# Two MoE layers behind attention: constant products at the layer border, GpSimd's weight splits moved to VectorE, the exact pass's condition moved forward, two copies per small block left out

## Chip, cores and metric

One core of a Trainium2 chip runs the whole program. The metric is the device time of one execution in microseconds (us); less is better. The kernel before was timed in three runs.

## What is computed

The reference, cut: causal attention over 4 x 12 heads of 448 tokens of width 64 gives a matrix x of 1792 tokens x 768. Two mixture-of-experts layers follow, each with 8 experts of a 768 x 1024 and a 1024 x 768 matrix.

```python
def moe(x, w_gate, w1, w2):            # first layer
    logits = x @ w_gate
    expert_idx = argmax(logits, axis=1)
    gate_w = softmax(logits)[arange(N), expert_idx]
    for e in range(E):
        mask = expert_idx == e
        out[mask] = gate_w[mask, None] * (relu(x[mask] @ w1[e]) @ w2[e])

def moe2(x, w_gate, w1, w2):           # second layer
    logits = x @ w_gate
    cap = N // E                       # 224 tokens an expert
    for idx in argsort(-logits.flatten()):
        tok, e = idx // E, idx % E
        if assigned[tok] >= 0 or counts[e] >= cap: continue
        assigned[tok] = e; counts[e] += 1
    for e in range(E):
        mask = assigned == e
        out[mask] = relu(x[mask] @ w1[e]) @ w2[e]
```

The second layer hands out tokens greedily, in the order of all 14336 logits, until each expert holds 224.

## The kernel before

The program has three stages on one core: `attention` (to about 225 us), `moe1` (the first layer, line 119 on) and `moe2` (the second layer, line 477 on).

**Weights.** Each float32 matrix is used as a sum of two parts in a reduced format: `split` (L171 and L172 in the first layer, L773 and L774 in the second) lets ScalarE copy a loaded 128-row chunk to a high part and another engine subtract it for the low part. A product of two such operands is three matmuls: high by high, high by low, low by high. The chunks are loaded by SyncE into 8 raw buffers; a split frees its buffer and issues the load of the chunk 8 further on. In `moe1` and in most of `moe2` VectorE does the subtraction. In `moe2` GpSimd does it for four chunks of the second matrix of the first expert in order (p = 0, odd k from KD on, L774).

**First layer.** Tokens are grouped by expert. A full block has 128 rows: `take` transposes gathered rows (with ScalarE and VectorE making the parts xh and xl of `xx`), `up`, `relu`, `transp_h`, `down`, and the tail functions `tail0` to `tail3` of the block before (logits for the next layer, scatter of its rows), which are issued between the products. How many rows an expert has is a value that all engines read, and blocks are behind conditions (L380, L387, L403). Where an expert leaves at most HB = 64 rows over, `small` (L305) is used. It holds 64 rows in 128 columns of the stationary operand: columns 0 to 63 the high part, columns 64 to 127 the low part, so that `pair` (L312) needs two matmuls where a block needs three, and `fold` and `transp_s` add the halves. The low part comes there by two VectorE copies at its start (L308, L309). `small` then issues weight splits by the list SPS = (5, 0, 2, 0, 3, 4, 0) between its pieces; the first five stand ahead of everything but the copies. In this trace it runs four times, from about 268, 394, 440 and 462 us.

**Border.** Ahead of the first layer nine matmuls of 512 columns with constant operands stand on TensorE (L417, `WARM`); their result is not used. Behind the last expert come the tails of the last block (L444 to L474), by which the second layer's logits get complete.

**Second layer.** The greedy order is found by thresholds: `search` (L627) takes four rounds for each expert in order, each a comparison on VectorE (`probe`, L622), 14 small matmuls (L665), a reduction (L666, L668), one matmul (L676) and the new thresholds; `assign` (L694) makes the index list of the expert by further small matmuls (L711, L725, L729). Both are one generator, `phases` (L735), whose pieces are placed by hand between the products: `go(n)` runs n pieces, `turn` runs one whenever the costs in the list `YY` say that it is due, `finish(p)` all that is left for an expert. For p = 0 nothing stands beside it but the first splits. Then `gather` (L781) fetches the expert's rows, `take` (L800) transposes them, `up4` (L822) makes the first four column tiles chunk by chunk as weights arrive, `up` (L815) the others, `relu` (L827, L828), `down` (L838), `put` (L785) scatters rows to the output. The splits of p + 1's first matrix and its `take` stand between the `down` products of p, by the list s0.

**Exact pass.** Ties can defeat the thresholds; each search adds to `bad` if so. At the very end VectorE turns `bad` into a flag (L918), every engine reads it (L921), and under a condition (L922) the whole layer is done again with exact ranks. The last output scatter, `put_half` (L791), is issued ahead of it.

The lines the text speaks of most:

```python
for s in (slice(0, 1), slice(1, KD)):                                             # L308
    nc.vector.tensor_copy(xh[:, s, HB:], xl[:, s, :HB])                           # L309
ops = [(o, a[:, k], wh, k == 0, k == n - 1), (o[:HB], a[:, k, :HB], wl, False, False)]
(nc.gpsimd if p == 0 and k >= KD and k % 2 else V).tensor_sub(l, r, h.bitcast(F32))  # L774
```

Of the kernel before, what the change touches and what calls it, by code (L numbers as in the profile page):

```python
# [119 lines left out]
def moe1(tc, w1, w2, wg, xs, y2, l2, ident, before, iob, cr, gt, g0, raw, early, iok, L, srch):  # L120
    nc = tc.nc
    with ExitStack() as c:
# [182 lines left out]
        def small(e, j):  # L305

            W = (w1h[e % 2], w1l[e % 2])
            for s in (slice(0, 1), slice(1, KD)):  # L308
                nc.vector.tensor_copy(xh[:, s, HB:], xl[:, s, :HB])  # L309
# [132 lines left out]
        for e in range(E):  # L442
            expert(e)

# [14 lines left out]
        tail1()  # L459
        for n in range(2):  # L460
            nc.tensor.transpose(pU[0][:, n * 128:n * 128 + 128], d[:, n:n + 1].to_broadcast([128, 128]), ident)
        tail2()

# [6 lines left out]
        tail3(False)  # L470
        V.tensor_mul(rh.rearrange("p (i e) -> p i e", e=E), oi[:, :, None].to_broadcast([128, NB, E]),
                     l2c[:, None, :].to_broadcast([128, NB, E]))
        nc.tensor.matmul(pU[1][:, :NB * E], hp, rh, start=True, stop=True)
        V.tensor_add(L, L, pU[1][:, :NB * E].rearrange("p (i e) -> p i e", e=E))  # L474


def moe2(tc, w1, w2, y2, out, ident, before, ones, io8, iok, iob16, L, srch, raw, force):
# [7 lines left out]
    with ExitStack() as c:  # L485
# [50 lines left out]
        iob = io8[:, None, :].to_broadcast([128, PT, E])  # L536

# [87 lines left out]
        def search(p):  # L625
# [61 lines left out]
            t = total()  # L687

# [6 lines left out]
        def assign(p):  # L695
# [14 lines left out]
            nc.tensor.matmul(t[:, :1], before, T["rt"], start=True, stop=True)  # L710
            V.tensor_copy(T["col"], t[:, :1])  # L711
# [14 lines left out]
            V.tensor_scalar(T["ev"], t[:16, :NA], float(N), None, op0=OP.min)  # L726
            yield YY[9]
# [67 lines left out]

        def take(kk):
            t = ps.tile([128, 512], F32, name="w", bufs=6)[:, :2 * CAP].rearrange("p (k g t) -> p k g t", k=2, g=2)
# [10 lines left out]
        def up(f, h):  # L808
            if h == 0:
                U[f] = ps.tile([128, 512], F32, name="w", bufs=6)[:, :CAP]  # L810
            u = U[f]
            fs = slice(f * 128, (f + 1) * 128)
            for k in range(3 * h, 3 * h + 3):
                for n, (w, x) in enumerate(((w1h, xh), (w1l, xh), (w1h, xl))):
                    nc.tensor.matmul(u, w[:, k, fs], x[:, k], start=(k == 0 and n == 0), stop=(k == KD - 1 and n == 2))  # L815

        def up4(k):
            for f in range(4):
                if k == 0:
                    U[f] = ps.tile([128, 512], F32, name="w", bufs=6)[:, :CAP]  # L820
# [11 lines left out]
        def down(g, hf, f0, f1):  # L832
            if f0 == 0:
                Y[0] = ps.tile([128, 512], F32, name="w", bufs=6)[:G2, :384]
# [19 lines left out]

        go(1)
        split(0, 0)
        go(2)
# [8 lines left out]
        for f in range(4, KF):  # L866
# [7 lines left out]
            split(0, KD + f)  # L874
        for p in range(E):
            early = p > 0 and p + 1 in done
            if p:
# [3 lines left out]
                for f in range(KF):  # L881
# [3 lines left out]
                    turn(p, 1)  # L885
                    relu(f)
# [3 lines left out]
            for g in range(2):  # L890
                for hf in range(2):
                    for f in range(0, KF, 2):
                        down(g, hf, f, f + 2)
                        turn(p, 1)
                        if n == s0[0]:
                            finish(p + 1)
                            flush()
                        if p + 1 in done and not early:
# [15 lines left out]
                if p < E - 1 or g == 0:  # L914
                    put(p, g)


        V.tensor_scalar(T["bi"], bad, 0.0, None, op0=OP.not_equal)  # L918
        if force:
            V.memset(T["bi"], 1)  # L920
        again = nc.values_load(T["bi"][0:1, 0:1], min_val=0, max_val=1)  # L921
        with tc.If(again > 0):  # L922
            reset()
            for p in range(E):
                best()
                V.tensor_tensor(T["eq"], T["lm"], T["m"][:, :, None].to_broadcast([128, PT, E]), op=OP.is_equal)
                V.tensor_mul(T["eq"], T["eq"], iob)
                V.tensor_reduce(T["mn"], T["eq"], axis=AX.X, op=OP.min)
                V.tensor_tensor(T["oh"], iob, T["mn"][:, :, None].to_broadcast([128, PT, E]), op=OP.is_equal)
                exact()  # L930
                owned()
                V.scalar_tensor_tensor(apen, T["asg"], -BIG, apen, op0=OP.mult, op1=OP.add)
                V.memset(T["fl"], 0.0)
                V.scalar_tensor_tensor(T["full"], cap, 0.0, left, op0=OP.is_equal, op1=OP.mult)
                for _ in assign(p):
                    pass
                gather(p)
                pend.clear()
                for k in range(NC):
                    load(p, k)  # L940
                    r = raw[(p * NC + k) % NR]
                    if k < KD:
                        h, l = w1h[:, k], w1l[:, k]
                    else:
                        r, h, l = r[:, :DM], w2h[:, k - KD], w2l[:, k - KD]
                    A.activation(h, r, AF.Copy)
                    V.tensor_sub(l, r, h.bitcast(F32))
                for kk in range(0, KD, 2):
                    take(kk)
                for f in range(KF):  # L950
                    up(f, 0)
                    up(f, 1)
                    relu(f)
                for g in range(2):
                    for hf in range(2):
                        down(g, hf, 0, KF)
# [339 lines left out]
```

## Time and profile before

| what | value |
|---|---|
| three runs | 986.0, 988.75, 988.78 us; median 988.75 |
| the profiled execution, its own time | 990.98 us |
| its span, first to last instruction | 989.1 us |
| mean granted TensorE clock over the span | 0.945 |
| busy: PE, PEld, DVE, ACT, POOL | 891.8, 744.1, 629.1, 503.1, 215.4 us |
| share of the chain that ended last: PE, DVE, DMA | 27%, 3%, 2% |

PE is TensorE's matmul pipe, PEld its weight loads, DVE VectorE, ACT ScalarE, POOL GpSimd, SP SyncE; a name with q is the engine's instruction queue. The durations are from one profiled execution, whose time is 1.9 us over its span. The chain's shares are of the whole span but the chain is followed back only to 625.87 us, so 27% of PE is most of what it covers. [...] Where a row says x8 it stands for eight instructions one after another; what stands in brackets is the idle time of the engine before it and what ended it.

### The profile page before, as it was taken

The page shows a single profiled execution, that of the slowest core. Times are in us where ns is not written, and L with a number is a line of the kernel's source. Part 1 is how long each engine was busy: PE and PEld are TensorE (multiplying, and loading weights), DVE is VectorE, ACT ScalarE, POOL GpSimd, SP SyncE. Part 2 cuts the span into 40 slices and gives each one's busy share as a digit, 9 for nine tenths or more (in the row PEclk, how much of TensorE's full clock was granted, in tenths as well). Part 3 has the DMA queues.
Part 4 walks back from the last instruction along what each step waited for, and adds up shares of the span by engine and source line. Part 5 has one row for each costly group of instructions (what it writes and reads, how often), then busy time and mean ns, then how long its engine had stood idle before and what let it go on. Part 6 is the DMA issues. An engine that isn't in the chain of part 4 may idle for free. (4 is left out here: it accounts for less than half of the span.)

```text
span 989.1 us, 18118 instructions
## 1 busy us (share of the span) xinstructions
PE 891.8 (90%) x6122; PEld 744.1 (75%) x6122; DVE 629.1 (64%) x1815; ACT 503.1 (51%) x1101; POOL 215.4 (22%) x244
## 2 busy tenths in 40 slices
PE   5999999995899996987999999458999999999993
PEld 3666666663778885766798878348899999999993
DVE  6888989868552613853821152578797887975640
ACT  5888888854563524654822253033444444445540
POOL 5555444404121111111211112104111011011001
PEclk9999999996999998998999999757999999999997
DMA  8654555706743803873831031074685766766701
GB/s 174 132 148 118 144 138 119 251 11 206 269 146 132 305 34 103 289 290 112 301 152 49 33 101 50 22 244 139 188 246 171 218 190 182 222 199 199 256 16 31
DMA packets 76911, 156.54 MB, mean 158 GB/s; under 512 B 30753, under 2 KB 41793, under 8 KB 76738
## 3 DMA queue, kind: packets, MB, share of 16 engines
q1 hardware_dynamic: 70514, 128.44, 42.2%
q0 software_dynamic: 6224, 26.11, 8.1%
q8 instruction: 70, 1.15, 0.5%
q14 instruction: 103, 0.84, 0.3%
HBM read 135.84 MB, written 18.67 MB: 156 GB/s over the span
## 5 line engine op out<-in xcount | busy, mean ns | idle before, releaser
L202 PE MATMUL pU<-w1h,xx 128*128 128x512 f32 x336 | 120.8, 414 | 9.0 <-DVE xx L256 2.9
L1037 ACT ACTIVATE p<-p,nm 112x112 f32<-112x112 f32 x192 | 99.8, 522 | 14.5 <-DVE nm L1030 14.2
L815 PE MATMUL w<-xh,w1h 128*128 128x224 f32 x360 | 102.1, 284 | 0.0
L815 PE MATMUL w<-xl,w1h 128*128 128x224 f32 x360 | 99.2, 276 | 0.3 <-DVE xl L804 0.3
L815 PE MATMUL w<-xh,w1l 128*128 128x224 f32 x360 | 98.8, 275 | 0.0
L1030 DVE CUSTOM_DVE_ANT_0 p<-s,msk 112x112 f32<-112x112 f32 x192 | 83.3, 440 | 12.9 <-PE s L1026 11.7
L838 PE MATMUL w<-w2h,hh 128*112 128x384 f32 x256 | 91.2, 356 | 0.0
L838 PE MATMUL w<-w2h,hl 128*112 128x384 f32 x256 | 88.0, 344 | 0.0
L838 PE MATMUL w<-w2l,hh 128*112 128x384 f32 x256 | 87.7, 342 | 0.3 <-DVE w2l L774 0.3
L202 PEld LDWEIGHTS pU<-w1h,xx 128*128 128x128 f32 x336 | 63.9, 191 | 27.0 <-issue 5.4
L1025 PE MATMUL s<-kh,qs 128*112 128x112 f32 x192 | 73.8, 384 | 10.4 <-DVE kh L1013 6.1
L1046 PE MATMUL t<-ident,p 112*112 112x112 f32 x480 | 80.3, 267 | 1.4 <-ACT pt L1051 0.8
L1008 POOL TENSOR_TENSOR qs<-qr,qs 64x448 fp32r<-64x448 f32 x44 | 54.3, 1253 | 82.4 <-ACT qs L1007 62.9
L815 PEld LDWEIGHTS w<-xl,w1h 128*128 128x128 f32 x360 | 69.1, 192 | 0.5 <-DVE xl L804 0.5
L815 PEld LDWEIGHTS w<-xh,w1h 128*128 128x128 f32 x360 | 69.0, 192 | 0.5
L815 PEld LDWEIGHTS w<-xh,w1l 128*128 128x128 f32 x360 | 69.1, 192 | 0.0
L172 DVE TENSOR_TENSOR w2l<-raw,w2h 128x768 fp32r<-128x768 f32 x64 | 58.2, 953 | 16.8 <-ACT w2h L171 14.5
L202 PE MATMUL pU<-w1l,xx 128*128 128x512 f32 x168 | 67.0, 399 | 0.0
L1057 PE MATMUL o<-pt,vt 112*64 112x336 f32 (+3 forms) x384 | 66.3, 424 | 0.0
L827 ACT ACTIVATE hh<-w 128x224 fp32r<-128x224 f32 x64 | 22.9, 358 | 84.5 <-PE w L815 63.7
L172 DVE TENSOR_TENSOR w1l<-raw,w1h 128x1024 fp32r<-128x1024 f32 x46 | 54.2, 1225 | 18.2 <-ACT w1h L171 13.5
L785 POOL DMA_INDIRECT out_dram<-yo,idx x15 | 15.3, 1021 | 231.2 <-ACT yo L841 203.0
(308 smaller groups left out, 2236.0 us busy)
## 6 DMA issues: line engine op xcount, KB each, us to landing
raw<-in_moe_w_dram SPq DMA_DIRECT2D x96, 512.0 KB
raw<-in_moe_w_dram SPq DMA_DIRECT2D x128, 384.0 KB
kr<-in_k_dram SPq DMA_DIRECT2D x46, 224.0 KB
qr<-in_q_dram SPq DMA_DIRECT2D x24, 224.0 KB
vt<-in_v_dram SPq DMA_DIRECT2D x48, 112.0 KB
xs<-xr SPq DMA_DIRECT2D x4, 1120.0 KB
xs<-xr SPq DMA_DIRECT2D x4, 238.0 KB
kr<-in_k_dram SPq DMA_DIRECT2D x4, 112.0 KB
```

The costliest lines, as they stand in the source:

```text
L172: (on or nc.vector).tensor_sub(l, r, h.bitcast(F32))
L202: nc.tensor.matmul(pU[half], a[:, k], w[:, k, cs], start=(m == 0), stop=(m == 17))
L785: nc.gpsimd.indirect_dma_start(out=out, out_offset=bass.IndirectOffsetOnAxis(ap=idx[p % 3][:, g:g + 1], axis=0), in_=yo[:, g], in_offset=None)
L815: nc.tensor.matmul(u, w[:, k, fs], x[:, k], start=(k == 0 and n == 0), stop=(k == KD - 1 and n == 2))
L827: A.activation(hh[:, f], u, AF.Relu)
L838: nc.tensor.matmul(y, a[:, f, g * G2:(g + 1) * G2], w[:, f, hf * 384:(hf + 1) * 384], start=(f == 0 and n == 0), stop=(f == KF - 1 and n = ...
L1008: (nc.gpsimd if u > 1 else nc.vector).tensor_sub(qs[64:], qr, qs[:64].bitcast(F32))
L1025: nc.tensor.matmul(s[:, :w], QS[u][:, h, i * Q:(i + 1) * Q], KH[u][:, h, :w], start=True, stop=False)
L1030: nc.vector.tensor_tensor_reduce(p, s[:, :w], msk[:, S - w:], scale=-0.125, scalar=3.0e38, op0=OP.add, op1=OP.min, accum_out=nm)
L1037: nc.scalar.activation(p, p, AF.Exp, bias=RS[u, "m"][:, h, i:i + 1], scale=-1.0, accum_out=RS[u][:, h, i:i + 1])
L1046: nc.tensor.transpose(t[:, k], P[u, h][:, o + k * Q:o + (k + 1) * Q], ident[:Q, :Q])
L1057: nc.tensor.matmul(OPS[u][h * 64:(h + 1) * 64, k * Q:], VT[u][:, h, k], PT[u, h][:, k, k * Q:], start=(k == 0), stop=(k == NQ - 1))
```

## The change

(1) `small` no longer has the two copies; its other lines stand as they were. (2) Constant products: `warm(n)` issues n matmuls of 512 columns on operands that never change, with a result that nobody reads, three times two and then four in the tails of the first layer, and in the second layer behind the small matmuls of the first expert's search and index, and ahead of its `take`. (3) `split` always subtracts on VectorE. (4) The exact pass is moved: `judge` sets the flag and lets all engines read it behind the fifth group of down products of the last expert but one, and `redo`, with the condition and the old body, stands in the last expert behind its first column tile. What can't be redone from there (the last expert's own products) is left to the ordinary code behind it, so the body stops after that tile. It needs PSUM tiles of its own, which `wt` and `alt` hand out.

```diff
         def small(e, j):
             W = (w1h[e % 2], w1l[e % 2])
-            for s in (slice(0, 1), slice(1, KD)):
-                nc.vector.tensor_copy(xh[:, s, HB:], xl[:, s, :HB])
             sp = begin(e, j, gf[:, e + 1:e + 2])
...
+        def warm(n):
+            for _ in range(n):
+                nc.tensor.matmul(pU[1], before, iob[:, None, :].to_broadcast([128, 4, 128]), start=True, stop=True)
...
         tail1()
+        warm(2)
...
         tail2()
+        warm(2)
...
         tail3(False)
+        warm(2)
...
         V.tensor_add(L, L, pU[1][:, :NB * E].rearrange("p (i e) -> p i e", e=E))
+        for _ in range(4):
+            nc.tensor.matmul(pU[0], before, iob[:, None, :].to_broadcast([128, 4, 128]), start=True, stop=True)
...
+        wz = ps.tile([128, 512], F32, name="w", bufs=6)
+        def warm(n):
+            for _ in range(n):
+                nc.tensor.matmul(wz, before, iob16[:, None, :].to_broadcast([128, 4, 128]), start=True, stop=True)
...
                 V.tensor_tensor_reduce(T["d"][:TH], t[:TH], T["capm"][:TH], scale=1.0, scalar=-3.0e38,
                                        op0=OP.subtract, op1=OP.max, accum_out=T["mx"][:TH])
+                if p == 0:
+                    warm(2)
...
                 nc.tensor.matmul(t[:, :1], ones[:TH], T["ok"][:TH], start=True, stop=True)
+                if p == 0:
+                    warm(4 if r < RN - 1 else 5)
...
             t = total()
+            if p == 0:
+                warm(5)
...
             nc.tensor.matmul(t[:, :1], before, T["rt"], start=True, stop=True)
+            if p == 0:
+                warm(6)
...
             V.tensor_scalar(T["ev"], t[:16, :NA], float(N), None, op0=OP.min)
+            if p == 0:
+                warm(2)
...
-            (nc.gpsimd if p == 0 and k >= KD and k % 2 else V).tensor_sub(l, r, h.bitcast(F32))
+            V.tensor_sub(l, r, h.bitcast(F32))
...
+        warm(7)
         go(1)
+        warm(2)
         split(0, 0)
-        go(2)
+        go(1)
+        warm(4)
+        go(1)
+        warm(5)
         split(0, 1)
         for kk in range(0, KD, 2):
             take(kk)
...
+        def judge():
+            finish(E - 1)
+            V.tensor_scalar(T["bi"], bad, 0.0, None, op0=OP.not_equal)
+            if force:
+                V.memset(T["bi"], 1)
+            verdict.append(nc.values_load(T["bi"][0:1, 0:1], min_val=0, max_val=1))
+            tc.mark_branch_hint_location("again", verdict[0] > 0, engines=list(nc.engines))
+        def redo():
+            u0 = U[0]
+            alt.extend([ps.tile([128, 512], F32, name="w", bufs=6) for _ in range(4)])
+            with tc.If(verdict[0] > 0, label="again"):
+                reset()
+                for p in range(E):
...
+                    if last:
+                        U[0] = u0
+                        up(0, 0, True)
+                        up(0, 1, True)
+                        break
...
+            alt.clear()
...
                     up(f, 1)
                     turn(p, 1)
+                    if p == E - 1 and f == 0:
+                        redo()
                     relu(f)
                     split(p, KD + f)
...
+                        if p == E - 2 and n == 4:
+                            judge()
...
-        V.tensor_scalar(T["bi"], bad, 0.0, None, op0=OP.not_equal)
...
-        again = nc.values_load(T["bi"][0:1, 0:1], min_val=0, max_val=1)
-        with tc.If(again > 0):
-            reset()
...
```

In `take`, `up`, `up4` and `down` the PSUM tile now comes from `wt()`, which outside the exact pass is the tile of before.

## Rows read from the trace of the kernel before

**Rows 1.** The page's part 2, TensorE's granted clock in 40 slices of 24.7 us.

```profile
PEclk9999999996999998998999999757999999999997
```

**Rows 2.** Windows: stretch, us, busy us (xcount) by engine, clock, DMA share, GB/s.

```profile
440.80:444.20 3.40, 3.40 (x12) 2.61 (x11) 0.42 (x1) 0.60 (x1) 0.00 (x0) 0.50 0.82 321
632.00:655.00 23.00, 5.41 (x93) 4.18 (x93) 18.20 (x85) 2.11 (x2) 2.27 (x7) 0.50 0.39 129
687.30:696.80 9.50, 9.19 (x39) 7.41 (x39) 6.87 (x18) 0.00 (x0) 3.98 (x7) 0.50 0.57 164
907.00:974.00 67.00, 67.00 (x494) 66.52 (x492) 31.25 (x45) 28.80 (x50) 6.65 (x7) 1.00 0.41 129
```

**Rows 3.** Line L403's branches at two small blocks: min/median/max ns, start us.

```profile
L403 PEldq COMPARE_BRANCH  x1: 75/75/75, 392.4 to 392.4; - x1
...
L403 PEldq COMPARE_BRANCH  x1: 70/70/70, 457.6 to 457.6; - x1
L403 DVEq COMPARE_BRANCH  x1: 64/64/64, 461.3 to 461.3; - x1
```

**Rows 4.** Timeline of the small blocks: start us, us, instruction, idle before and releaser.

```profile
394.25 0.76 PE L316 MATMUL pU<-w1h,xx 128*128 128x512 f32 x1 [7.17 <-DVE xx L309]
...
440.03 0.48 PE L316 MATMUL pU<-w1h,xx 128*128 128x512 f32 x1 [2.43 <-DVE xx L309]
...
461.93 0.77 PE L316 MATMUL pU<-w1h,xx 128*128 128x512 f32 x1 [4.96 <-DVE xx L309]
...
466.87 0.42 DVE L231 COPY yb<-pB 128x256 f32<-128x256 f32 x1
...
469.79 0.43 PE L236 MATMUL pA<-hb,wg 128*32 128x128 f32 x8
```

**Rows 5.** Timeline from 231 us, the constant products of the first layer.

```profile
231.19 4.02 PE L417 MATMUL pU<-iob,before 128*128 128x512 bf16 x9 [0.55 <-DVE gt L1194]
```

**Rows 6.** The chain that ended last, 640 to 690 us: start us, us, what.

```profile
648.74 6.34 DMA xg<-y,idx
...
655.12 2.33 PE w L800 x11
...
659.17 2.83 PE w L822 x12
662.01 0.57 PE gp L665 x14
...
674.28 1.44 PE w L822 x12
...
678.74 0.44 PE gp L725 x14
```

**Rows 7.** Timeline of PE ahead of the first take, 650 to 656 us.

```profile
651.00 0.18 PE L676 MATMUL gp<-t_ok,ones 40*128 40x1 bf16 x1 [1.44 <-DVE t_ok L668]
...
652.89 0.42 PE L800 MATMUL w<-ident,xg 112*128 112x112 f32 x1 [1.70 <-DMA xg<-y,idx]
```

**Rows 8.** Timeline of 673 to 716 us, GpSimd's splits and PE's wait.

```profile
679.93 3.65 POOL L774 TENSOR_TENSOR w2l<-raw,w2h 128x768 fp32r<-128x768 f32 x2 [30.03 <-ACT w2h L773]
...
687.36 0.63 PE L665 MATMUL gp<-t_oh,t_g 128*40 128x8 bf16 x14 [2.64 <-DVE t_g L622]
```

**Rows 9.** VectorE's t_lm and t_g, all of them: min/median/max ns, first to last start.

```profile
L616 DVE TENSOR_TENSOR t_lm<-L,t_pen x7: 274/275/1875, 646.5 to 872.7; 128x112 f32<-128x112 f32 x7
...
L622 DVE TENSOR_TENSOR t_g<-t_mm,srch x28: 741/742/2273, 630.9 to 849.4; 128x560 bf16<-128x560 f32 x28
```

**Rows 10.** VectorE's groups by form, 640 to 990 us: busy us, mean ns, idle before.

```profile
L774 DVE TENSOR_TENSOR w2l<-raw,w2h 128x768 fp32r<-128x768 f32 x60 | 57.1, 951 | 7.6 <-ACT w2h L773 7.4
```

**Rows 11.** Line L922, the condition at the end: ns, start us.

```profile
L922 PEldq COMPARE_BRANCH  x1: 3616/3616/3616, 971.5 to 971.5; - x1
...
L922 POOLq INC_SWDGE_SEM  x1: 1932/1932/1932, 979.0 to 979.0; - x1
```

**Rows 12.** Timeline of PE at a skipped condition in the first layer, 578 to 580.5 us.

```profile
579.89 0.61 PE L220 MATMUL pY<-w2h,hh 128*128 128x384 f32 x2 [0.63 <-PEq L381]
```

More of the change, by code (lines that the diff above doesn't have):

```diff
@@ L794, in put_half, with wt @@
                 in_=yo[:, g, h * 384:(h + 1) * 384], in_offset=None)
+        alt = []
+        def wt():
+            if alt:
+                alt.append(alt.pop(0))
+                return alt[-1]
+            return ps.tile([128, 512], F32, name="w", bufs=6)
         def take(kk):
-            t = ps.tile([128, 512], F32, name="w", bufs=6)[:, :2 * CAP].rearrange("p (k g t) -> p k g t", k=2, g=2)
+            t = wt()[:, :2 * CAP].rearrange("p (k g t) -> p k g t", k=2, g=2)
             for k in range(2):
@@ L806, in moe2, with up @@
         U = {}
-        def up(f, h):
-            if h == 0:
-                U[f] = ps.tile([128, 512], F32, name="w", bufs=6)[:, :CAP]
+        def up(f, h, again=False):
+            if h == 0 and not again:
+                U[f] = wt()[:, :CAP]
             u = U[f]
@@ L819, in up4 @@
                 if k == 0:
-                    U[f] = ps.tile([128, 512], F32, name="w", bufs=6)[:, :CAP]
+                    U[f] = wt()[:, :CAP]
                 for n, (w, x) in enumerate(((w1h, xh), (w1l, xh), (w1h, xl))):
@@ L833, in down @@
             if f0 == 0:
-                Y[0] = ps.tile([128, 512], F32, name="w", bufs=6)[:G2, :384]
+                Y[0] = wt()[:G2, :384]
             y = Y[0]
@@ L874, in moe2 @@
             split(0, KD + f)
+        def judge():
[11 more added lines that the diff above has]
+                for p in range(E):
+                    best()
+                    V.tensor_tensor(T["eq"], T["lm"], T["m"][:, :, None].to_broadcast([128, PT, E]), op=OP.is_equal)
+                    V.tensor_mul(T["eq"], T["eq"], iob)
+                    V.tensor_reduce(T["mn"], T["eq"], axis=AX.X, op=OP.min)
+                    V.tensor_tensor(T["oh"], iob, T["mn"][:, :, None].to_broadcast([128, PT, E]), op=OP.is_equal)
+                    exact()
+                    owned()
+                    V.scalar_tensor_tensor(apen, T["asg"], -BIG, apen, op0=OP.mult, op1=OP.add)
+                    V.memset(T["fl"], 0.0)
+                    V.scalar_tensor_tensor(T["full"], cap, 0.0, left, op0=OP.is_equal, op1=OP.mult)
+                    for _ in assign(p):
+                        pass
+                    gather(p)
+                    last = p == E - 1
+                    for k in range(NC):
+                        load(p, k)
+                        if last and k >= KD:
+                            continue
+                        r = raw[(p * NC + k) % NR]
+                        if k < KD:
+                            h, l = w1h[:, k], w1l[:, k]
+                        else:
+                            r, h, l = r[:, :DM], w2h[:, k - KD], w2l[:, k - KD]
+                        A.activation(h, r, AF.Copy)
+                        V.tensor_sub(l, r, h.bitcast(F32))
+                    for kk in range(0, KD, 2):
+                        take(kk)
+                    if last:
[3 more added lines that the diff above has]
+                        break
+                    for f in range(KF):
+                        up(f, 0)
+                        up(f, 1)
+                        relu(f)
+                    for g in range(2):
+                        for hf in range(2):
+                            down(g, hf, 0, KF)
+                        put(p, g)
+            alt.clear()
@@ L875, in moe2 @@
+        verdict = []
         for p in range(E):
@@ L914, in moe2 @@
                 if p < E - 1 or g == 0:
-                    put(p, g)
-        V.tensor_scalar(T["bi"], bad, 0.0, None, op0=OP.not_equal)
-        if force:
-            V.memset(T["bi"], 1)
-        again = nc.values_load(T["bi"][0:1, 0:1], min_val=0, max_val=1)
-        with tc.If(again > 0):
-            reset()
[L924 to L956, printed above, removed]
                     put(p, g)
```

## The prediction

> **What bounds the kernel now.** I read the page first, for TensorE's granted clock by slice; then tables of stretches; then what PE waits for in the first MoE layer; then the chain and the timelines of the few stretches where PE is not full. The clock row [rows 1] has dents in slice 10 (the first layer's start), 16 and 19 (its middle) and 26 to 28 (the border of the two layers). Nearly everywhere else PE is the bound: from 907 to 974 us, which hold the last two experts, it is busy for all of 67 us at full clock [rows 2]. So a microsecond won before that stretch is one won at the end, unless a DMA or VectorE is close behind. Three parts of this change lie in or behind the dents, the fourth behind the last product.
>
> **Small blocks, two copies each.** PE waited three times for the copies of L309, 7.17, 2.43 and 4.96 us [rows 4]. The copies themselves take half a microsecond; what PE waits for is VectorE getting there. In the block at 457 PE has passed its branch at 457.6, VectorE only at 461.3 [rows 3]. Without the copies PE's first product needs nothing that VectorE does in this block and can start at about 457.9 instead of 461.93: 4.0 sooner. But the second layer's gate products (L236, 469.79) need yb, which VectorE writes from 466.87 on [rows 4], behind the five weight splits that SPS puts ahead of it. VectorE gains only its own half microsecond, so those products start near 466.8, 3.0 sooner, after an idle time of PE in which the clock may fall; that would take half of it back. I take 1.5. In the block at 394 PE passed its branch at 392.4 [rows 3] and starts 1.8 sooner; 2.0 with a clock that rises sooner. In the block at 440 VectorE had weight splits ahead of the copies; PE starts about 1.9 sooner, and the half clock of 440.8 to 444.2, 3.4 us full of products [rows 2] of which 1.7 are lost, has no idle time left ahead of it: 3.6. In the fourth block the wait ends with ScalarE, and I give it 0.5. Sum **-7.5** (rounded). Bounds: -1.5, if only VectorE's half microseconds count three times, and -10.5, if every start is kept (4.0 + 1.8 + 1.9 + 0.5), with the clock's 1.7 and half a microsecond beside it. The diff has no new slice in the products: they read the 128 columns of xh as before. Read so or in two runs of 64, the columns are as many; I cost it at nothing, with 0 to 1 as its bounds.
>
> **Constant products.** That they can lift the clock the trace shows: nine of them take 4.02 us at half clock [rows 5], 0.45 each, so 0.22 at full. From 632 on the clock is at half, with PE busy 5.4 of 23 us [rows 2]. The groups of 2 to 7 stand in gaps of PE that VectorE makes; at full clock 2 take 0.45 and 6 take 1.3, and only two gaps are too narrow (ahead of the last gate transpose and of the index product): +0.3. A group of 14 small products takes 0.57 at half clock and 0.44 at full [rows 6]; over six groups -0.8. Take has eleven transposes in 2.33 at half clock [rows 6]; ScalarE and VectorE behind them set the pace when PE is faster: -0.7. The large sum would be up4: twelve products take 2.83 at half and 1.44 at full [rows 6], five times, some 7 us on PE, of which VectorE's splits between the groups would leave about 4. But the constant products end before the gather lands. Its DMA takes 6.34 us, to 655.1 [rows 6]; the last five products stand behind the search product of 651.0 and end near 652.2, and until 655.1 PE has one transpose [rows 7]. After PE's 2.64 us of idle at 684.7 [rows 8] the clock stayed at half for 9.5 us [rows 2]. So I expect it to fall again just ahead of up4, which then runs as now. **-1.2**. Bounds: -5 (the clock holds) and +5 (it is at half all through; groups of 2, 4 and 5 then take 0.9, 1.8 and 2.2 and overrun their gaps by 0.3 to 0.9, over four rounds).
>
> **Four weight splits from GpSimd to VectorE.** The trace has what they do now. GpSimd takes 3.65 us for two of them [rows 8], and a second pair follows. Under the first VectorE's t_lm takes 1.88 instead of 0.28, under the second its t_g 2.27 instead of 0.74 [rows 9], and the next small step is held as well. PE waits 2.64 for t_g [rows 8] and then runs at half clock to 696.8 [rows 2]. In their place VectorE gets four splits of 0.95 [rows 10], two ahead of the search of expert 2 and two behind it. Laid out one after another: expert 1's index at 681.4, two splits to 682.7, t_g done at 685.3 (now 687.3), then relu and split in turn, the last split done at 691.0. PE starts the search product at 685.3, waits about 1.9 for the fourth split and 0.2 for the third, and has its first 24 down products done near 691.9; now that is the end of the stretch at half clock, 696.8. That is -5; a fall of the clock in the new wait, one chance in three, gives back 1.7. **-4.5**. Bounds: -6.5 (no wait for the splits) and -1.5 (half clock as now). GpSimd is then free to issue expert 1's gather as soon as its index stands, some 7 us sooner, and the weight loads gated behind it follow; nothing becomes late by that.
>
> **The moved condition.** At the end it takes away GpSimd's semaphore step of 1.93 us [rows 11] ahead of the last drain; the last output scatter is not held by the condition. With the wait for that scatter partly beside it I take -2.5 (0 to -4). In its new place every engine loads a flag that VectorE wrote half an expert earlier and skips a long body. Queued behind it are: on PE the rest of the last expert's up products; on ScalarE and VectorE relu(0) and the splits, needed when the down products begin, some 16 us later; on SyncE nothing, its loads are all issued; on GpSimd the scatters near the end. Over the same body PE's branch took 3.6 us at the end [rows 11], but it is issued ahead of products that still run: at such a skip in the first layer PE idled 0.63 [rows 12]. I take +0.8 (0 to 3.6). **-1.7**. [...]
>
> **Sum.** -7.5 - 1.2 - 4.5 - 1.7 = -14.9. The profiled execution has a span of 989.1 and a time of its own of 990.98; the median of the runs, 988.75, lies 2.2 under that. Taken off the median: 973.9, so **974.0**.
>
> **The rivals.** (a) The clock holds through the gather's wait. For it: the constant products keep PE fuller than anything there now. Against: the nearly empty 2.9 us named above. Another -4: 970. (b) The small blocks give VectorE's half microseconds alone, because yb and the end of each block are paced by its splits. For it: the five splits ahead of yb. Against: at 440 nothing is queued behind its start. The 7.5 shrinks to 1.5: 980. (c) The constant products find the clock low and stand in the way, +5 where I have -1.2: 980. For it: transposes and tiny products are all that PE has there. Against: slice 25 is still at full clock [rows 1], so the groups begin warm. (d) On the other side: the condition is true and the exact pass runs. Its place is the branch in the last expert; its price is at least eight passes at the pace of [rows 2], 8 x 67 / 2 = 268 us; the time is 1240 or more. It decides as soon as one search ends without a threshold that fits. For it: by the diff as it stands the small blocks' first products lose the low parts, so the next layer's logits move. Against: moved logits still separate, and in this profile the body was skipped. (e) The change does not do all it says, the two-run read not being in the diff. The time is then the forecast's.
>
> **How the numbers follow.** Forecast 0.58, from 968 to 980 by the bounds of its terms, (e) being inside it; (a) 0.16, (b) 0.14, (c) 0.07, (d) 0.02; 0.03 is left for a price of the branch that eats most of the gain. The range from 965 to 983 takes in (a), (b) and (c) with a spread of their own and leaves out less than 0.2. About 0.3%, 3 us, is what a measurement of this kernel can tell from no change. Faster 0.94, same 0.03, slower 0.03.
>
> **What would show it.** Right: no wait of PE for L309, and its first product of a small block within half a microsecond of its branch; clock at full from 632 to about 655 and at half in up4; no t_g over 0.8 us and no split on GpSimd; PE's idle time at 684.7 under 1 us; one gap of PE under 1 us early in the last expert; the last drain some 2 us closer to the last product. Wrong: up4 at full clock (a); new waits of PE inside the small blocks as long as those that went (b); search rounds longer than now (c); 3 us or more at the moved branch.

## The result, and the profile after

The median went from 988.76 us (four runs, 986.0 to 990.77) to **976.24** (four runs, 973.63 to 977.49): a ratio of 0.987, interval 0.984 to 0.990. The forecast was 974.0, from 965 to 983. The profiled execution of the changed kernel took 973.63, with a span of 971.8. That is 17.3 less than the span of before where the medians differ by 12.5, so a stretch is judged below by several traces.

The page's row of the granted clock, which answers to [rows 1]; a slice is now 24.3 us:

```profile
PEclk9999999997999999899999999978999999999998
```

Three dents at the border have become two (slices 27 and 28), of the middle ones one is left; slice 40 is the end. Windows of the changed kernel, with the columns of [rows 2]:

```profile
458.10:464.90 6.80, 6.24 (x23) 4.76 (x24) 3.65 (x8) 3.28 (x5) 1.95 (x2) 0.50 0.99 380
622.00:642.00 20.00, 16.51 (x144) 7.12 (x142) 16.68 (x84) 2.11 (x2) 2.27 (x7) 1.00 0.29 97
642.40:662.90 20.50, 17.13 (x108) 14.41 (x107) 14.79 (x50) 5.42 (x7) 0.00 (x0) 0.50 0.63 213
676.31:686.50 10.19, 8.64 (x58) 7.16 (x57) 7.58 (x22) 1.49 (x3) 0.35 (x4) 1.00 0.83 275
```

The border is at full clock (1.00 in its window) until 642, with PE busy 16.5 of 20 us where it was 5.4 of 23; the first four column tiles still run at half clock (0.50); the first down products, at half clock before, are at full. In PE's timeline of the changed kernel a product of 224 columns starts 0.21 us behind the one before it at half clock (L855 at 651 us) and 0.11 at full (L848 at 671 us).

The table gives the length of stretches in us, each from the start or end of a named instruction in the timelines. First layer: first constant product of L417 to the last down product. Border: from there to the end of `up4`. Rest: on to the next `take`. Half: the start of the last transpose of the last `take` to the last expert's first down product. Tail: behind the last product. What is left of a span (attention, the middle, the last down products) differs by less than 2 us between any two.

| run | median | first layer | border | rest | half | tail |
|---|---|---|---|---|---|---|
| before | 988.76 | 394.0 | 50.6 | 31.9 | 16.2 | 15.0 |
| changed | 976.24 | 384.9 | 49.9 | 27.1 | 18.0 | 10.0 |
| copies_back | 982.59 | 392.0 | 49.7 | 28.6 | 19.8 | 10.0 |
| before_no_copies | 981.70 | 384.6 | 49.8 | 31.8 | 16.2 | 15.1 |
| dummy_copies | 976.95 | 391.6 | 49.8 | 28.7 | 17.9 | 10.0 |
| no_constant | 978.03 | 388.3 | 49.9 | 28.6 | 18.0 | 10.0 |
| constant_longer | 975.50 | 386.8 | 49.6 | 28.7 | 18.0 | 10.0 |
| constant_fill | 972.47 | 387.4 | 45.4 | 27.1 | 17.9 | 10.0 |
| gpsimd_splits_back | 981.01 | 393.4 | 49.9 | 32.0 | 18.0 | 10.0 |
| condition_at_end | 978.41 | 388.0 | 50.0 | 28.7 | 16.2 | 14.7 |
| hint_near | 978.28 | 387.5 | 49.9 | 28.6 | 19.8 | 10.0 |
| fill_interleaved | 973.76 | 387.6 | 45.4 | 27.1 | 19.8 | 10.0 |
| fill_condition_later | 966.24 | 384.5 | 45.4 | 27.1 | 16.7 | 10.0 |
| whole_computation | 968.76 | 384.9 | 46.1 | 28.6 | 16.7 | 10.0 |

The first layer differs most from trace to trace: eight other kernels with the changed kernel's code there (those from no_constant to hint_near, fill_condition_later and before_no_copies) have 384.5 to 393.4 in their one trace each. Its length is PE's busy and idle time. Windows of the first layer in the changed kernel, in copies_back and in dummy_copies (both below):

```profile
231.45:616.34 384.89, 357.55 (x2041) 301.16 (x2041) 179.45 (x319) 176.89 (x294) 68.10 (x65) 0.96 0.46 162
231.53:623.58 392.05, 359.06 (x2041) 302.90 (x2041) 181.26 (x327) 176.71 (x294) 65.13 (x65) 0.96 0.46 159
230.52:622.10 391.58, 361.71 (x2041) 305.31 (x2041) 181.32 (x327) 176.84 (x294) 64.44 (x65) 0.95 0.46 159
```

PE is idle for 27.3, 33.0 and 29.9 us of these stretches (length less busy time), and the granted clock is at half for 28.7, 32.6 and 39.3; in these three the busy time grows with the time at half clock (357.6, 359.1 and 361.7). Over all traces the idle time is 33.0 and 33.3 where PE waits for the copies (copies_back and before), and 26.9 to 29.9 in eleven of the twelve others (32.4 in gpsimd_splits_back). The time at half clock does not sort by the copies: 32.6 and 35.5 with them, 26.0 to 39.3 without. The other columns of the table repeat far better, on a few levels.

### The profile page after: what moved, and what is told of

Its sections match the earlier page's. It is cut to its first block, busy times and chain, and to the rows that moved or that the text cites. A ratio compares the mean times of both kernels' runs of the same rounds, so it can differ in the third digit from the quotient of the medians.

```text
span 971.8 us, 18237 instructions
## 1 busy us (share of the span) xinstructions
PE 900.8 (93%) x6188; PEld 743.1 (76%) x6188; DVE 625.6 (64%) x1811; ACT 503.3 (52%) x1101; POOL 207.0 (21%) x240
## 5 line engine op out<-in xcount | busy, mean ns | idle before, releaser
L848 PE MATMUL w<-xh,w1h 128*128 128x224 f32 x360 | 102.4, 284 | 0.3 <-PEq L926 0.3
L848 PE MATMUL w<-xh,w1l 128*128 128x224 f32 x360 | 98.9, 275 | 1.0 <-DVEq L926 1.0
L848 PE MATMUL w<-xl,w1h 128*128 128x224 f32 x360 | 99.0, 275 | 0.3 <-DVE xl L837 0.3
L848 PEld LDWEIGHTS w<-xh,w1l 128*128 128x128 f32 x360 | 69.0, 192 | 1.1 <-DVEq L926 1.1
L848 PEld LDWEIGHTS w<-xh,w1h 128*128 128x128 f32 x360 | 69.0, 192 | 1.0 <-issue 0.5
L848 PEld LDWEIGHTS w<-xl,w1h 128*128 128x128 f32 x360 | 69.1, 192 | 0.5 <-DVE xl L837 0.5
L172 DVE TENSOR_TENSOR w2l<-raw,w2h 128x768 fp32r<-128x768 f32 x64 | 58.2, 954 | 14.2 <-ACT w2h L171 12.8
L799 DVE TENSOR_TENSOR w2l<-raw,w2h 128x768 fp32r<-128x768 f32 x64 | 60.8, 951 | 8.2 <-ACT w2h L798 8.0
```

Of the source, the lines that this page charges most:

```text
L172: (on or nc.vector).tensor_sub(l, r, h.bitcast(F32))
```

## The experiments

In the changed kernel a small block's first products read the high parts only; the low parts of its rows are left out. That holds for every run below except copies_back, fill_interleaved and whole_computation.

**The two copies.** copies_back puts L308 and L309 of before back:

```diff
             W = (w1h[e % 2], w1l[e % 2])
+            for s in (slice(0, 1), slice(1, KD)):
+                nc.vector.tensor_copy(xh[:, s, HB:], xl[:, s, :HB])
```

> The changed kernel with the two copies per small block put back; all else as changed. Theory (the wait): TensorE waits for VectorE to reach the copies, and that wait is what the change removed; the first layer ends 8.9 us later than in the changed kernel, the time goes from 976 to 984 or 985, and the three waits of TensorE on the copies are back at 7, 2 and 5 us. Rival (VectorE's time): only VectorE's own half microseconds count, so the time is 977 to 978.

dummy_copies has the same two lines, with `xl[:, s, HB:]` as their destination.

> The changed kernel with the same two VectorE copies at the same place, written to columns of the low part's tile that no product of a small block reads. VectorE does all that it did before, TensorE does not wait for it. Theory (the wait): within 1.5 us of the changed kernel, 976 to 977.5. Rival (VectorE's time): as slow as with the real copies.

before_no_copies takes the two lines out of the kernel before and changes nothing else.

> The kernel before with nothing changed but the two copies per small block left out (so the low part of a small block's rows is not in its first product, as in the changed kernel). Theory (the waits, and the clock behind them): the first layer takes 385 to 388 us in the trace instead of 394, and the time falls by 6 to 9 us, to 980 to 983. Rival (the gain of the changed kernel's first layer is a lucky trace): 1.5 to 3 us, 986 to 987.

Measured, as ratios to the kernel before: copies_back 0.9935 (0.9917 to 0.9953), dummy_copies 0.9877 (0.9844 to 0.991), before_no_copies 0.9938 (0.9917 to 0.9959). Put back into the changed kernel the copies cost 6.3 us (982.59 against 976.24); taken out of the kernel before they give 7.1. The first layer, expected 8.9 us longer in copies_back, was 7.2 longer. The same VectorE work that TensorE does not wait for costs 0.7, inside the spread (971.0 to 982.9), and its interval does not touch that of copies_back. Its traced run took 981.0 and is among its longest; the 391.6 us of its first layer come from the clock, with 6.7 us more at half than in copies_back and 3.1 us less of idle time. The wait is shown, rival (b) is out. PE's timeline in copies_back has the waits again (answering to [rows 4]):

```profile
268.80 0.48 PE L316 MATMUL pU<-w1h,xx 128*128 128x512 f32 x1 [2.72 <-DVE xx L309]
...
393.60 0.77 PE L316 MATMUL pU<-w1h,xx 128*128 128x512 f32 x1 [5.99 <-DVE xx L309]
...
440.23 0.48 PE L316 MATMUL pU<-w1h,xx 128*128 128x512 f32 x1 [1.15 <-DVE xx L309]
...
460.58 0.77 PE L316 MATMUL pU<-w1h,xx 128*128 128x512 f32 x1 [4.99 <-DVE xx L309]
```

and PE's timeline of the changed kernel has the first products of the same four blocks and, behind those of the last block, its gate products:

```profile
265.58 0.40 PE L314 MATMUL pU<-w1h,xx 128*128 128x512 f32 x1
...
389.78 0.76 PE L314 MATMUL pU<-w1h,xx 128*128 128x512 f32 x1 [5.68 <-ACT w2h L171]
...
433.40 0.40 PE L314 MATMUL pU<-w1h,xx 128*128 128x512 f32 x1
...
449.54 0.47 PE L314 MATMUL pU<-w1h,xx 128*128 128x512 f32 x1 [0.89 <-ACT hb L344]
...
458.66 0.64 PE L236 MATMUL pA<-yb,wg 128*32 128x128 f32 x4 [3.17 <-DVE yb L231]
```

Read the two together by the lead of the changed kernel over copies_back, at the last product ahead of each block and at the block's last down product: 0.3 to 3.3 us, 3.5 to 3.9, 5.5 to 6.9, 6.9 to 6.9. The first block gives 3.0, the second 0.4, the third 1.4, the fourth nothing. Another 1.6 arise between the second and the third, 1.4 of them in down products ahead of the third block, which copies_back runs at half clock (434.8 to 438.3). dummy_copies has a fall of the clock at that place too (433.7 to 437.1), so these 1.4 are not shown to come from the copies. The fourth block starts 4.1 us sooner in relation to what stands ahead of it, and gives all of it back: PE waits 3.17 for yb, which VectorE reaches only behind five weight splits, and runs at half clock from 458.1 to 464.9 (the first of the windows above). In the second block PE's wait has a new end. The view of its branches in the changed kernel:

```profile
L401 DVEq COMPARE_BRANCH  x1: 57/57/57, 389.5 to 389.5; - x1
L401 PEldq COMPARE_BRANCH  x1: 75/75/75, 389.5 to 389.5; - x1
```

PE comes to it no sooner than VectorE, so it would not have waited long for the copies here; the condition ahead, L387, held it (PE's branch there takes 4.38 us from 385.1, shown in the last section), and not the weights that the row names.

**Constant products.** no_constant issues none of the new ones; constant_longer has more ahead of the first `take`:

```diff
         go(1)
-        warm(2)
+        warm(5)
         split(0, 0)
         go(1)
-        warm(4)
+        warm(7)
         go(1)
-        warm(5)
+        warm(13)
         split(0, 1)
```

> The changed kernel without any of the new constant products (the nine of the first layer's start stay). Theory (the clock falls again in the gather's wait): TensorE is at half clock from the border on and the search rounds take what they took, 0.5 to 1.2 us more, 976.5 to 977.5. Rival 1 (they are worth more): 4 or more us slower, 980 and up. Rival 2 (they stand in the way): faster than the changed kernel by 1 us or more.

> The changed kernel with more constant products ahead of the first take: 5, 7 and 13 where it has 2, 4 and 5, so that TensorE has work until the gather lands. Theory: the clock stays at full through the wait, the take and the five groups of the first four column tiles; the groups of twelve take 1.4 instead of 2.8 us, VectorE's splits between them leave about 4 us of gain: 972. Rival (the splits set the pace of these groups): at full clock but with TensorE waiting for weights, 975 to 976. Rival (the clock falls all the same, at the take): 976, with the groups at half clock.

constant_fill adds more to constant_longer, behind the gather:

```diff
+                    if fill:
+                        warm(fill.pop())
...
-            go(2 if k < 3 else 1)
+            go(1)
+            if k < 3:
+                warm(2 if k else 6)
+                go(1)
...
             up4(k)
+            if k < 2:
+                warm(2)
```

> The kernel of the run constant_longer with further constant products in the gaps behind the gather: 3 between the two halves of the gather, 6 behind the transposes, 2 in each gap of the first search rounds and of the first two groups. In constant_longer the clock fell at 650.4 us, one round into the first four column tiles, behind the gap of TensorE that follows the transposes. Theory (the clock falls where TensorE has gaps): it now stays at full from the border through the five groups, which takes 3 to 4 us off the stretch of the groups (16.6 us in constant_longer), and the time is 972. Rival (VectorE's splits set the pace): the clock stays at full and the stretch still takes 15.5 us or more; the time is 974.5 or more.

Without any constant product the border is as long (49.9 both times). The median is 1.8 higher, with intervals that overlap (0.9875 to 0.9925 against 0.984 to 0.9903): no gain is shown in the stretch where they stand. constant_longer, then constant_fill, in windows:

```profile
642.00:650.40 8.40, 6.08 (x49) 3.53 (x46) 5.61 (x19) 3.11 (x5) 0.00 (x0) 1.00 0.94 330
650.40:664.00 13.60, 12.71 (x83) 12.05 (x81) 10.70 (x40) 2.08 (x3) 0.00 (x0) 0.50 0.48 153
```

```profile
643.40:647.50 4.10, 4.10 (x22) 1.81 (x20) 3.66 (x10) 0.00 (x0) 0.00 (x0) 1.00 0.91 274
647.50:660.30 12.80, 12.67 (x122) 9.18 (x120) 10.13 (x34) 5.19 (x7) 0.00 (x0) 1.00 0.74 267
```

With the gather's wait alone filled, the clock holds through it and falls at 650.4, behind the gap that follows the transposes; the theory named one gap too few, and the border stays 49.6. With the later gaps filled too, the clock holds through all of `up4`, and the border takes 45.4 us, 4.5 less than in the changed kernel. `up4` itself goes from 16.6 us in constant_longer to 12.7. The rival that VectorE's splits set the pace, with 15.5 us or more for `up4`, is out. The medians (972.47 against 976.24) agree in size, with wide intervals.

**GpSimd's splits.** One line, as it was:

```diff
-            V.tensor_sub(l, r, h.bitcast(F32))
+            (nc.gpsimd if p == 0 and k >= KD and k % 2 else V).tensor_sub(l, r, h.bitcast(F32))
```

> The changed kernel with the four splits of the first expert on GpSimd again. Theory (GpSimd and VectorE hinder each other): VectorE's t_lm and t_g take 1.9 and 2.3 us again, TensorE waits 2.6 us for t_g and half clock follows; the stretch from the end of the first four column tiles to the next take, 27.1 to 28.7 us in the traces of the kernels without GpSimd's splits, takes about 31.9 as before: 3 to 4.5 us slower, 979 to 981. Rival (the splits on VectorE cost as much as they save): within 1 us of the changed kernel.

Measured 981.01, ratio 0.9905 (0.9871 to 0.9938), and 32.0 us for the rest of the first expert. The interval overlaps that of the changed kernel (0.984 to 0.9903) a little, so the stretch decides, which is 27.1 to 28.7 us in every trace without GpSimd's splits. All t_lm and t_g of that run (the view of their lines), and in its timeline PE's wait, as in [rows 8, 9]:

```profile
L631 DVE TENSOR_TENSOR t_lm<-L,t_pen x7: 274/276/1870, 644.6 to 870.4; 128x112 f32<-128x112 f32 x7
...
L637 DVE TENSOR_TENSOR t_g<-t_mm,srch x28: 741/742/2262, 629.1 to 847.1; 128x560 bf16<-128x560 f32 x28
```

```profile
684.88 0.63 PE L680 MATMUL gp<-t_oh,t_g 128*40 128x8 bf16 x14 [2.63 <-DVE t_g L637]
```

and of the changed kernel, with PE's wait for the splits that VectorE now makes:

```profile
L631 DVE TENSOR_TENSOR t_lm<-L,t_pen x7: 274/275/276, 637.6 to 858.5; 128x112 f32<-128x112 f32 x7
...
L637 DVE TENSOR_TENSOR t_g<-t_mm,srch x28: 741/741/743, 622.1 to 835.2; 128x560 bf16<-128x560 f32 x28
```

```profile
679.77 0.43 PE L871 MATMUL w<-w2l,hh 128*112 128x384 f32 x1 [1.55 <-DVE w2l L799]
```

No t_lm or t_g is long any more, so GpSimd's work did hold VectorE: with the splits on GpSimd the longest t_lm takes 1.87 us against a median of 0.28, and the longest t_g 2.26 against 0.74. How GpSimd's work holds VectorE's no run here shows. The stretch has two levels, 27.1 and 28.6: in seven of the eleven traces without GpSimd's splits the clock fell for 3.4 us behind the new wait, in four it did not.

**The condition.** condition_at_end drops `judge` and `redo` and has the block of before at the end. hint_near leaves the condition where the change put it and issues its branch hint at the start of the last expert.

> The changed kernel with the condition of the exact pass back at the end, as before. By the forecast 1.7 us slower (2.5 at the end less 0.8 at the branch); by the trace of the changed kernel 3.2 slower: the stretch behind the last product 15.0 instead of 10.0 us, the last expert's first half 16.2 instead of 18.0. Theory: 3.2, so 979 to 980. Rival (the end is set by the last scatter's landing): less than 1 us, 976 to 977.

> The changed kernel with the branch hint issued at the start of the last expert instead of with the flag, half an expert earlier. In the changed kernel ScalarE and GpSimd pass the condition in 0.5 us and VectorE in 2.9, and TensorE's second product behind it waits for VectorE. Theory (the hint's place decides how long VectorE's skip takes): VectorE passes in under 1 us and the last expert's first half takes 17 instead of 18 us; 975. Rival (the hint's place does not matter): 18 us as now, 976. Rival (a late hint comes too late): 18 us or more, with longer skips on the other engines.

By the stretches the condition at the end costs 14.7 - 10.0 = 4.7 us in the tail and saves 18.0 - 16.2 = 1.8 in the half, 2.9 in all; the median differs by 2.2 (978.41), with intervals that overlap. GpSimd's last scatter and its final drain, in the kernel before and then in the changed one (each time the timeline of POOL, then the view of the program's last line, in ns):

```profile
975.82 0.94 POOL L791 DMA_INDIRECT out_dram<-yo,idh  x1 [3.57 <-PEq L922]
```

```profile
L1292 POOLq DRAIN  x3: 50/114/7339, 980.9 to 988.8; - x3
```

```profile
962.71 0.94 POOL L816 DMA_INDIRECT out_dram<-yo,idh  x1 [3.03 <-ACT yo L874]
```

```profile
L1352 POOLq DRAIN  x3: 46/120/8519, 962.5 to 971.6; - x3
```

Before, the drain began at 980.9, 5.1 us behind the scatter's start; now it begins at 962.5 with the scatter and runs beside its landing. The scatter itself starts 1.7 us behind the end of the last product (974.14) before, put down to PE's branch at L922, and 0.9 behind it (961.84) now: 0.8 of the 5.0 us. The new price is at the branch. The view of line L926 and PE's timeline behind it, changed kernel:

```profile
L926 DVEq COMPARE_BRANCH  x1: 80/80/80, 927.9 to 927.9; - x1
L926 PEldq COMPARE_BRANCH  x1: 360/360/360, 928.5 to 928.5; - x1
...
L926 DVEq EVENT_SEMAPHORE  x1: 21/21/21, 930.8 to 930.8; - x1
```

```profile
929.54 0.34 PE L848 MATMUL w<-xh,w1h 128*128 128x224 f32 x1 [0.30 <-PEq L926]
...
930.83 0.37 PE L848 MATMUL w<-xh,w1l 128*128 128x224 f32 x1 [0.96 <-DVEq L926]
```

PE's own skip costs it 0.30 of idle time; then its second product, which reads w1l, waits 0.96 until VectorE, which would write w1l in the body, is past the body. VectorE needs 2.9 us for that. It had needed 2.8 at the end of the kernel before (960.2 to 963.0), where PE's products ran on (the view of L922):

```profile
L922 DVEq COMPARE_BRANCH  x1: 68/68/68, 960.2 to 960.2; - x1
...
L922 DVEq EVENT_SEMAPHORE  x1: 21/21/21, 963.0 to 963.0; - x1
```

With the hint near, ScalarE needs 3.0 too, where it needed 0.6 in the changed kernel (the view of the condition's line in hint_near):

```profile
L925 ACTq COMPARE_BRANCH  x1: 59/59/59, 931.4 to 931.4; - x1
...
L925 ACTq EVENT_SEMAPHORE  x1: 17/17/17, 934.4 to 934.4; - x1
```

and VectorE 2.9 as ever (932.1 to 935.0), so the theory on the hint fell. The half took 19.8 there, but 1.8 of it is a fall of the clock that copies_back and fill_interleaved have too, with the hint at its old place; 978.28 shows no difference.

fill_condition_later moves the condition behind the second column tile, in constant_fill, with VectorE's and ScalarE's work for the first tile behind it (the body then makes both tiles again, and has three PSUM tiles of its own, not four):

```diff
-                    if p == E - 1 and f == 0:
-                        redo()
+                    if p == E - 1 and f == 0:
+                        continue
+                    if p == E - 1 and f == 1:
+                        redo()
+                        relu(0)
+                        split(p, KD)
                     relu(f)
```

> The kernel of the run constant_fill with the condition of the exact pass behind the second column tile of the last expert instead of the first, and VectorE's and ScalarE's work for the first tile behind it, so that VectorE reaches the condition while TensorE still has 2 us of products. Theory (TensorE waits for VectorE's skip of 2.9 us, not for its own): the wait of 0.96 us on VectorE goes, the last expert's first half takes 16.6 to 17.0 instead of 17.9 us; 971.5. Rival (VectorE's skip starts later by as much): 17.9 as now, 972.5.

The view of the condition's line in this run, and PE's timeline behind it:

```profile
L934 DVEq COMPARE_BRANCH  x1: 80/80/80, 921.7 to 921.7; - x1
L934 PEldq COMPARE_BRANCH  x1: 365/365/365, 922.9 to 922.9; - x1
L934 DVEq EVENT_SEMAPHORE  x1: 21/21/21, 924.7 to 924.7; - x1
```

```profile
925.37 0.34 PE L851 MATMUL w<-xh,w1h 128*128 128x224 f32 x1 [0.30 <-PEq L934]
```

VectorE is past at 924.7, PE needs it behind 925.4 and waits only for itself. The half takes 16.7, 1.2 less than in constant_fill, which shows what the wait was worth; 0.5 more than with the condition at the end is left. The median, 966.24 (963.15 to 969.04), fell by 6.2; the trace has 2.9 of it in the first layer, whose code is the same, and I have no cause for that part.

**All of the computation.** fill_interleaved puts high and low part of each row side by side, in constant_fill (its other lines add the halves accordingly and apply the gate weight behind the second product):

```diff
-        xx = sm.tile([128, KD, 2, 128], F32R, name="xx")
-        xh, xl = xx[:, :, 0], xx[:, :, 1]
+        xx = sm.tile([128, KD, 128, 2], F32R, name="xx")
+        xh, xl = xx[:, :, :, 0], xx[:, :, :, 1]
+        x2 = xx.rearrange("p k t s -> p k (t s)")
...
-                    pair(pU[half], xh, W[0][:, k, cs], W[1][:, k, cs], k, KD)
+                    for n, w in enumerate(W):
+                        nc.tensor.matmul(pU[half], x2[:, k, :128], w[:, k, cs], start=(k == 0 and n == 0),
+                                         stop=(k == KD - 1 and n == 1))
```

> The kernel of the run constant_fill with the whole computation kept in the small blocks and still no copies: the tile of the rows' two parts holds high and low part of each row side by side, so that a small block reads both in one run of 128 columns and full blocks read theirs with a step of two; the halves are added by a matrix that sums neighbouring rows, and the gate weight is applied behind the second product. Theory (a step of two costs TensorE's weight loads nothing): within 2 us of constant_fill, 971 to 975, with the weight loads of the first layer's first products at 191 ns. Rival (a load with a step takes longer than its product): at twice 191 ns the 504 products of full blocks would be paced by loads at 382 instead of 217 ns, up to 80 us more. Rival (ScalarE and VectorE write with a step more slowly): some 0.3 us more for each block's transposes, 4 to 6 us.

It took 973.76 (971.28 to 977.13), ratio 0.985 as constant_fill. The weight loads of the first products in the groups by line, 225 to 620 us, in constant_fill and then in fill_interleaved:

```profile
L202 PEld LDWEIGHTS pU<-w1h,xx 128*128 128x128 f32 x336 | 64.4, 193 | 26.7 <-issue 5.0 <-DVE sin L369 3.7 <-DVE xx L256 3.3
...
L204 PEld LDWEIGHTS pU<-w1h,xx 128*128 128x128 f32 x336 | 67.0, 200 | 24.7 <-issue 5.1 <-DVE sin L374 3.2 <-DVE xx L258 3.0
```

A load of 200 ns against 193: the step of two costs nothing that the time shows. whole_computation joins this with the later condition.

> The interleaved rows of fill_interleaved and the later condition of fill_condition_later in one kernel: the whole computation of the kernel before, without copies. Theory (both are what their stretches show, interleaving costs nothing, the later condition takes 1.2 us off the last expert's first half of constant_fill): 967 to 972, with 16.8 us for that half. Rival (interleaving costs 0.3 us per block, hidden in fill_interleaved by the spread of its runs): 972 to 976.

968.76 (967.73 to 970.96), ratio 0.9793 (0.9769 to 0.9816), half 16.7: faster than both kernels, with nothing left out.

## Why the prediction was right

The time and its direction were right. That the time came within 2.2 us is in part luck: three terms promised too much and the fourth too little. The terms, one by one:

- **Small blocks, -7.5.** The runs give -6.3 and -7.1. The mechanism was right, the sum 0.4 to 1.2 too large, and its parts were not right: 0.5, 2.0, 3.6 and 1.5 forecast for the four blocks in order of time, 3.0, 0.4, 1.4 and nothing seen in the pair of traces (and 2.2 outside the blocks, 1.4 of them a fall of the clock). The step that failed is each block's wait read from one trace: which engine is last at a block's start, and where the clock falls, changes from one trace to the next. For the fourth block the mechanism was foreseen (yb behind the splits, then half clock), its price was put at half of the gain and was all.
- **Constant products, -1.2.** 0.0 in the stretch. That the clock falls ahead of `up4` was right, and rival (a) needs more than it named: with the clock held through the gather's wait alone (constant_longer) the border is 0.3 shorter, and only with the gaps behind it filled too (constant_fill) come the 4 us it promised, 4.5. The groups of small products and the transposes, from which the 1.2 came, are not what sets the border's length. That VectorE's search and the gather do is argued and not tested: VectorE is busy for 16.7 of the 20 us from 622 in the changed kernel, PE's products being at full clock there, and the border is no shorter than in no_constant, at half clock. The clock did rise behind constant products: in the changed kernel it is 0.50 over the nine of L415 (231.45 to 235.47, 0.45 us each) and 0.95 from 236.2 to 240. Of the new ones at full clock two take 0.60 us and four 1.04, so 0.22 for one more.
- **Splits, -4.5.** -3.3 or -4.8, by whether the clock falls in the new wait. The wait for the fourth split was forecast at 1.9 and was 1.55. The chance of a fall was put at one in three; it was seven traces of eleven, so -3.3 was the likelier entry.
- **The condition, -1.7.** -3.2 by the traces, both parts mis-sized: -2.5 at the end was -5.0, beyond its bound of -4, and +0.8 at the branch was +1.8. The first failed in "the wait for that scatter partly beside it": not only the semaphore step goes, the drain of 7 us begins with the scatter instead of 5 us behind its start. It also took the last scatter as "not held by the condition", where the trace of the kernel before ends the scatter's wait with PE's branch at L922; it now starts 0.8 us closer to the last product. The second failed in the list of what is queued behind the branch: relu and the splits were counted as VectorE's only dependents, and not the weights w1l, which the skipped body could write and PE's next product reads. The forecast priced PE's skip alone; VectorE's 2.8 us at L922 stood in the same trace. What VectorE does in the 2.9 us that it stood at L926 no run here shows; PE's branch there took 0.36 us.

Rival (d) did not occur, the body was skipped. Rival (e) holds: no two-run read is in the code. A read in two runs was not tried; fill_interleaved shows that a read of both parts, laid side by side, costs nothing that can be measured (973.76 us against 972.47, loads of 200 ns against 193).

By the runs the sum is about -6.5, 0, -3.3 and -2.9, -12.7 in all, against -12.5 measured. What stays open: why PE's idle time and the falls of the clock in the first layer differ between traces of the same code (by up to 9 us of its length), and the 1.8 us by which no_constant's median is higher.

## What to carry to other kernels

When an instruction that makes an engine wait is taken out, look for the next one on the same queue: here VectorE's lateness came back as a wait for yb (3.17 us). Of a skipped condition, count what the slowest engine needs to skip it, if an instruction of the bound engine close behind reads anything that the body writes on that engine: here VectorE needed 2.9 us, TensorE waited 0.96 for it, and it was worth 1.2 us to place the condition where VectorE arrives early. Constant products paid here only when they reached across every gap up to the work that they were to speed up (border 45.4 us in constant_fill, 49.6 in constant_longer).

## What the runs showed of the hardware

A skipped body did not cost all engines alike: at L926 of the changed kernel ScalarE 0.6 us, PE's branch 0.36, VectorE 2.9. Nor did one condition cost the same in two runs of the same code. The branch L387 in the changed kernel, then in gpsimd_splits_back:

```profile
L387 PEldq COMPARE_BRANCH  x1: 4379/4379/4379, 385.1 to 385.1; - x1
```

```profile
L387 PEldq COMPARE_BRANCH  x1: 5159/5159/5159, 388.9 to 388.9; - x1
```

GpSimd's final drain got longer (8.5 instead of 7.3 us), and still ended 8.3 us behind the start of the last scatter instead of 12.4, because it began with it.
